# Moving the softmax shares' copies from ScalarE to GpSimd, starting the key and query splits one tile earlier, and giving the folded weights their own buffer

## The chip, the cores and the metric

The kernel runs on one core of a Trainium2 chip. The metric is device time in microseconds (us) of the whole program: the median of several runs. TensorE (PE) multiplies and transposes, VectorE (DVE) and ScalarE (ACT) read its results from PSUM, GpSimd (POOL) works on SBUF only, and nearly all transfers are issued by SyncE (SP), one after the other in program order.

## The reference

Three layers follow each other. The change lies in the work done during the first one.

```python
# 1: attention, B=4, H=8, S=1152, D=64; two queries are averaged into one
q_pool = q.reshape(B, H, S // 2, 2, D).mean(axis=3)
scores = scale * q_pool @ k^T
attn = exp(scores - max) / (sum + 1e-9)
x = (attn @ v) rearranged to (B, 576, 512)
# 2: four single-head causal attentions ("experts") on x, the best two per token mixed
ye = softmax(causal(scale * (x wq_e)(x wk_e)^T)) @ (x wv_e) @ wo_e
out = sum of the two chosen experts, weighted
# 3: gate = sigmoid(causal depthwise convolution of out, 5 taps)
result = (gate * (out @ w_val)) @ w_out
```

Everything is float32. A product that must keep more than the short float format holds is done with each operand split into a high part and a low part (the rest), both in the format that TensorE multiplies fast; those are the "splits" below.

## The kernel before

**Stage 1** is the first layer. It runs over 16 pairs of heads; a pair has nine tiles of 128 query rows in two units: unit 0 has the tiles `(u, i)` = (0, 0) to (0, 3), unit 1 has (1, 0) to (1, 4). One loop runs over all 144 tiles, and in a pass each engine gets work of several tiles: TensorE the scores of tile m+1 (L406) and the transposes of the probabilities of tile m-2 (L451); VectorE the row minimum of tile m+1 (L411); ScalarE the exponential of tile m (L417) and two of the three evacuations of the transposes (`pt`, L459), VectorE the third (L461). The transposes have two PSUM buffers, so the third group of a tile waits until ScalarE has emptied the first. Every engine works its instructions off in the order of the program.

When a unit's last tile is through, `shares` (L419) takes the reciprocals of the row sums (`rs`, L426 and L427) and spreads them into the tile `rm`, which has one buffer. One pass later `av` transposes `rm` (L438; a small matmul at L440 for the fifth tile's shares), ScalarE copies the result to `rb` (L472), TensorE runs 36 matmuls of probabilities by values (L476), and VectorE multiplies by `rb` (`xf`, L478). During these 36 matmuls the loop calls `between`, which also gives VectorE a stretch of decoding work (below).

**GpSimd's work in stage 1** comes from four sources, in this order within a pass: the list `late` (steps put off by an earlier pass, run at the head of the next), then one step of `prep`, then what `between` calls, then one step of `bgw`.

- `prep(n + 1)` makes the next pair's operands. It adds the two query halves (`qp`, L385), splits keys in three groups (`hlk`: high part L362, low part L363) and queries (`hlq`, L378 to L380). Its four steps run in four successive passes; low parts go to `late`. Then SP moves the splits into place (`kmove`, twelve transfers in three groups, and `qmove`, six).
- `av` puts the split of its result (`xt`, L485 and L481) on `late`; SP then stores it in `x_d`.
- `dense_weights` (iterator `bg`) decodes the third layer's weights on VectorE, with one addition on GpSimd (L103), and splits them on GpSimd into the tile `whl`, which SP stores in `w_d` (`w3_d`).
- `bgw` is `expert_weights` and then `folded_weights`: SP fetches a block of weights into `wst`, GpSimd splits it (L136, L138). `folded_weights` handles four blocks of the transposed output weights `wo_t`, into the same tile `whl` (L156, L157), stored in `wot_d`. The pool of `whl` has one buffer.

SP issues the load of pair n+2 (`kt`, `qt`, `vn`) in the pass of tile (1, 2). `kt` and `qt` have one buffer each.

**Stages 2 and 3** are the other layers. They begin at about 541 us and the change does not touch them.

Of the kernel before, what the change touches and what calls it, by code (L numbers as in the profile page):

```python
# [10 lines left out]
F32R = mybir.dt.float32r  # L11
I32 = mybir.dt.int32
AF = mybir.ActivationFunctionType
ALU = mybir.AluOpType
# [6 lines left out]
def tile_kernel(ctx, tc, q, k, v, w_gate, wq, wk, wv, wo, w_val, conv_w, w_out, wo_t, out):  # L21
    nc = tc.nc
    B, H, S, D = v.shape
    P = 128
# [9 lines left out]
    scale = 1.0 / math.sqrt(D)  # L34
    pe, act, dve, pool = nc.tensor, nc.scalar, nc.vector, nc.gpsimd
# [28 lines left out]
    def f(ap):  # L64
        return ap.bitcast(F32)
# [14 lines left out]
    HW = DM // 2  # L80
# [27 lines left out]
    def expert_weights(raws):  # L108

        ED = E * D  # L110
        todo = []
        for n, w in enumerate((wq, wk, wv)):
            for t in range(KT):
                dst = wqk if n < 2 else wvg
                cs = slice((n % 2) * ED, (n % 2) * ED + ED)
                todo.append((dst[0][:, t, cs], dst[1][:, t, cs], w[:, t * P:(t + 1) * P, :].rearrange("e p d -> p e d"), ED))
        for t in range(KT):
            todo.append((wvg[0][:, t, ED:], wvg[1][:, t, ED:], w_gate[t * P:(t + 1) * P, :], E))
        for g in range(EP):
            todo.append((wos[0][:, g, :], wos[1][:, g, :], wo[2 * g:2 * g + 2].rearrange("two d m -> (two d) m"), DM))  # L120
        bufs = {}

        def fetch(j):
            if j < len(todo):
                hi, lo, src, width = todo[j]
                st = bufs[j] = raws.tile([P, DM], F32, name="wst")[:, 0:width]
                nc.sync.dma_start(st if len(src.shape) == 2 else st.rearrange("p (e d) -> p e d", e=E), src)

        fetch(0)
        yield  # L130
        yield
        for j, (hi, lo, src, width) in enumerate(todo):
            fetch(j + 1)
            yield
            st = bufs.pop(j)
            pool.tensor_copy(hi, st)  # L136
            yield
            pool.tensor_tensor(out=lo, in0=st, in1=f(hi), op=ALU.subtract)  # L138

    def folded_weights(stage, raws):  # L140

        bufs = {}

        def fetch(t):
            if t < KT:
                bufs[t] = raws.tile([P, DM], F32, name="wst")[:, 0:HW]
                nc.sync.dma_start(bufs[t], wo_t[t * P:(t + 1) * P, :])

        fetch(0)
        yield  # L150
        for t in range(KT):
            fetch(t + 1)
            yield
            raw = bufs.pop(t)
            whl = stage.tile([P, 2, HW], F32R, name="whl")
            pool.tensor_copy(whl[:, 0], raw)  # L156
            pool.tensor_tensor(out=whl[:, 1], in0=raw, in1=f(whl[:, 0]), op=ALU.subtract)  # L157
            late.append(lambda t=t, whl=whl: nc.sync.dma_start(f(wot_d[:, t]), f(whl)))
            yield

    def dense_weights(stage, raws):

        craw = stage.tile([P, KT, KC, 2], I32, name="craw")
        cw64 = conv_w.bitcast(I32).rearrange("k (t p two) -> p t k two", p=P, two=2)
        for t in range(KT):
            nc.sync.dma_start(craw[:, t], cw64[:, t])
        big = [(n, t, c, w[t * P:(t + 1) * P, c:c + HW].bitcast(I32)) for n, w in enumerate((w_val, w_out)) for t in range(KT) for c in (0, HW)]
        bufs = {}

        def fetch(j):  # L170
            if j < len(big):
                bufs[j] = raws.tile([P, 2 * HW], I32, name="wraw")
                nc.sync.dma_start(bufs[j], big[j][3])

        fetch(0)
        yield True
        yield from decode(stage, craw.rearrange("p t k two -> p (t k) two"), KT * KC, cw.rearrange("p t k -> p (t k)"))
        for j, (n, t, c, src) in enumerate(big):
            fetch(j + 1)
            w32 = yield from decode(stage, bufs.pop(j).rearrange("p (m two) -> p m two", two=2), HW)  # L180
            whl = stage.tile([P, 2, HW], F32R, name="whl")
            pool.tensor_copy(whl[:, 0], w32)
            pool.tensor_tensor(out=whl[:, 1], in0=w32, in1=f(whl[:, 0]), op=ALU.subtract)
            late.append(lambda n=n, t=t, c=c, whl=whl: nc.sync.dma_start(f(w3_d[n][:, t, :, c:c + HW]), f(whl)))
            yield
# [116 lines left out]
    with ExitStack() as s1:  # L302
# [20 lines left out]
        own = sums_p.tile([P, P], F32, name="own")  # L323
# [12 lines left out]
        pairs = [(b, hp) for b in range(B) for hp in range(H // 2)]  # L336
        data = {}

        def load(n):
            b, hp = pairs[n]  # L340
            kt = nat.tile([P, C * P], F32, name="kt")
            nc.sync.dma_start(kt, k[b, hp])
            qt = nat.tile([P, 2, SQ], F32, name="qt")
            nc.sync.dma_start(qt, q[b, hp])
            vn = v_p1.tile([P, 2, C, D], F32, name="vn")
            nc.sync.dma_start(vn, v[b, 2 * hp:2 * hp + 2].rearrange("h (p c) d -> p h c d", p=P))
            data[n] = [qt, kt, vn]

        late = []
# [69 lines left out]
        def shares(m):  # L419

            n, u, i, _ = tiles[m]
            k = len(UNITS[u])
            if i == k - 1:
                rs = st_p.tile([P, 5], F32, name="rs")[:, 0:k]
                rm = rss[n, u] = rb_p.tile([P, 3, P], F32, name="rm")
                dve.tensor_scalar(rs, sums[(2 * n + u) % len(sums)][:, 0:k], 1e-9, None, op0=ALU.add)  # L426
                dve.reciprocal(rs, rs)  # L427
                both = rs[:, 0:4].rearrange("p (h t) -> p t h", h=2)[:, :, :, None].to_broadcast([P, 2, 2, D])
                act.activation(rm[:, 0:2].rearrange("p t (h d) -> p t h d", d=D), both, AF.Copy)
                if u == 1:  # L430
                    act.activation(rm[:, 2], own, AF.Copy, scale=rs[:, 4:5])

        def spread_shares(n, u):

# [107 lines left out]
        for m in range(-1, M + LAG + 4):  # L542
# [22 lines left out]
                fill = proj(xh[0], 0) + fill  # L565
            if 0 <= m < M:
                n, u, i, _ = tiles[m]
                if (u, i) == (0, 1) and n + 1 < len(pairs):
                    preps = prep(n + 1)
                if (u, i) == (1, 2) and n + 2 < len(pairs):  # L570
                    load(n + 2)
                if m == 5:
                    bg, bgw = dense_weights(d_p, raw_p), chain(expert_weights(raw_p), folded_weights(d_p, raw_p))
# [3 lines left out]
            for what, g in ((0, 0), (1, 0), (0, 1), (1, 1), (0, 2), (1, 2)) if burst else ((0, 0), (0, 1), (1, 0), (0, 2), (1, 1), (1, 2)):  # L577
                if what == 0:
                    if 0 <= m - LAG < M:
                        transp(m - LAG, g)  # L580
                    if m >= M:
                        now2, late2[:] = late2[:], []
                        if fill:
                            fill.pop(0)[1]()
                        for a in now2:
                            a()
                        if urgent:
                            urgent.pop(0)()
                        if not fill and late2:
                            for a in late2:  # L590
                                a()
                            late2.clear()
                    if g == 1:
                        if m in (0, 1):
                            begin[m]()
                        if 0 <= m < M and m not in done:
                            expo(m)
                        if m in (2, 3):
                            begin[m]()
                    if g == 2:  # L600
                        if 0 <= m - 1 < M:
                            shares(m - 1)
                        if preps:
                            preps.pop(0)()
                elif 0 <= m + 1 < M:
                    scores(m + 1, g)
# [60 lines left out]
    with ExitStack() as s2l:  # L667
# [157 lines left out]
        def ahead(n):  # L825
            return (WORK[steps[n][2]][0] if n < len(steps) else 0) + (WORK[steps[n - LAG][2]][1] if LAG <= n < len(steps) + LAG else 0)
# [34 lines left out]
        for n in range(len(steps) + LAG):  # L861
            if n < len(steps):
                b, g, i = s = steps[n]
# [36 lines left out]
            t = 0.0  # L900
            left = 5 - n % 5
            own = [ahead(m) for m in range(n, n + left)]
# [71 lines left out]
    with ExitStack() as s3:  # L974
# [5 lines left out]
        both = gs_p.tile([P, KT, 2, 2 * SQ], F32R, name="gs")  # L980
# [95 lines left out]
```

## Time and profile before

| what | value |
|---|---|
| median of 3 runs | 824.21 us (824.21 to 825.62) |
| the profiled execution, its own time | 824.22 us |
| its span, first to last instruction | 822.4 us |
| PE, DVE, ACT, POOL busy | 94%, 67%, 59%, 35% of the span |
| mean granted TensorE clock | 0.992 of full speed |

The profiled execution is as long as the median, and 1.8 us of it lie outside the span. "Busy" is an average over the three stages; which engine sets the pace at a given moment is read from the waits.

### The profile page before, as it was taken

Reading aid. Unit: us, or ns where it says so; the run is one execution under the profiler, and the core shown is the slowest. Engines: PE = TensorE matmul, PEld = TensorE weight load, DVE = VectorE, ACT = ScalarE, POOL = GpSimd, SP = SyncE. Lnnn points to the kernel's source line nnn. Section 1 sums busy time; section 2 is a strip of 40 time slices with the busy share of each in tenths; the row PEclk is TensorE's granted clock in tenths of the full one; section 3 lists DMA queues with packets and bytes.
Section 4 is the critical chain, followed back from the end, with each engine's and each line's share of the span. In section 5 each row is a group of like instructions: output and inputs, shape, how many; then the busy total and the mean of one; then the engine's idle time right before and its main releaser. Section 6 shows DMA issues by size and latency. Waiting matters only on the chain.

```text
span 822.4 us, 14720 instructions
## 1 busy us (share of the span) xinstructions
PE 774.1 (94%) x5348; PEld 629.6 (77%) x5348; DVE 548.8 (67%) x998; ACT 489.2 (59%) x1072; POOL 290.2 (35%) x372
## 2 busy tenths in 40 slices
PE   5999999997999999999999999998999999988998
PEld 4777777775777776786777777887998989876887
DVE  4577777776677777566556645526569889897840
ACT  5676677564665676666666756624455464647542
POOL 3463763844546345244144240002222222220000
PEclk9999999999999999999999999998999999999999
DMA  7767778666696595773764857067345464810212
GB/s 228 170 199 221 203 205 246 174 206 178 190 274 170 174 271 135 197 217 89 215 162 119 230 125 253 15 153 202 88 91 180 106 203 116 234 71 1 77 65 89
DMA packets 86295, 134.49 MB, mean 164 GB/s; under 512 B 21584, under 2 KB 58960, under 8 KB 86224
## 3 DMA queue, kind: packets, MB, share of 16 engines
q1 hardware_dynamic: 86224, 133.57, 57.6%
q8 instruction: 42, 0.69, 0.4%
q14 instruction: 29, 0.24, 0.1%
HBM read 53.37 MB, written 21.76 MB: 91 GB/s over the span
## 4 chain that ended last, share of the span: by engine, by line
PE 65%; DVE 13%; ACT 12%; DMA 5%; SPq 2%; issue 2%; POOL 0%; ACTq 0%; DVEq 0%
PE t L476 17%; PE s L406 12%; PE t L451 10%; ACT p L417 6%; PE a L231 6%; PE o L992 6%; DVE nm L411 5%; PE a L262 4%; PE a L782 3%; ACT pt L459 2%; DVE pt L461 2%; PE s L684 2%; DMA xh<-x_d 2%; PE a L649 2%; PE a L756 1%
## 5 line engine op out<-in xcount | busy, mean ns | idle before, releaser
L451 PE MATMUL t<-ident,p 128*128 128x128 f32 x1296 | 207.6, 280 | 17.9 <-ACT pt L459 15.2
L411 DVE TENSOR_REDUCE nm<-s 128x1 f32<-128x1152 f32 x144 | 194.1, 1348 | 28.7 <-PE s L406 21.8
L459 ACT ACTIVATE pt<-t 128x384 f32<-128x384 f32 x288 | 132.3, 488 | 134.7 <-PE t L451 133.4
L451 PEld LDWEIGHTS t<-ident,p 128*128 128x128 f32 x1296 | 151.7, 142 | 65.3 <-ACT pt L459 29.4
L417 ACT ACTIVATE p<-s,nm 128x1152 f32<-128x1152 f32 x144 | 176.2, 1224 | 37.7 <-DVE nm L411 33.5
L476 PE MATMUL t<-pt,vn 128*64 128x320 f32 (+1 forms) x1152 | 146.8, 408 | 0.0
L406 PE MATMUL s<-ka,qst 128*128 128x384 f32 x480 | 129.6, 373 | 13.3 <-ACT ka L523 6.9
L406 PE MATMUL s<-kb,qst 128*128 128x384 f32 x480 | 132.4, 368 | 2.0 <-ACT p L417 1.4
L461 DVE COPY pt<-t 128x384 f32<-128x384 f32 x144 | 80.4, 558 | 75.4 <-PE t L451 72.9
L476 PEld LDWEIGHTS t<-pt,vn 128*64 128x64 f32 x1152 | 80.0, 137 | 54.2 <-issue 2.7
L406 PEld LDWEIGHTS s<-ka,qst 128*128 128x128 f32 x480 | 78.5, 194 | 21.6 <-ACT p L417 8.7
L406 PEld LDWEIGHTS s<-kb,qst 128*128 128x128 f32 x480 | 77.4, 191 | 5.1 <-ACT p L417 2.0
L720 POOL TENSOR_TENSOR p<-p,sm 128x512 f32<-128x512 f32 (+3 forms) x32 | 40.2, 1255 | 114.3 <-DVE sm L718 85.2
L231 PE MATMUL a<-xh,wqk 128*128 128x288 f32 x384 | 59.7, 306 | 2.5 <-DVE pt L734 2.1
L478 DVE TENSOR_TENSOR xf<-t,rb 128x256 f32<-128x256 f32 (+1 forms) x32 | 14.6, 457 | 68.1 <-PE t L476 67.6
L485 POOL CAST xt<-xf 128x256 fp32r<-128x256 f32 (+1 forms) x32 | 13.6, 424 | 129.0 <-DVE xf L478 128.9
L231 PEld LDWEIGHTS a<-xh,wqk 128*128 128x128 f32 x384 | 54.5, 194 | 4.1 <-DVE pt L734 2.5
L363 POOL TENSOR_TENSOR hlk<-kt,hlk 128x384 fp32r<-128x384 f32 x45 | 45.4, 1010 | 2.2
L705 ACT ACTIVATE p<-s,nm 128x256 f32<-128x256 f32 (+3 forms) x64 | 33.1, 524 | 21.7 <-DVE nm L694 21.7
L385 POOL TENSOR_TENSOR qp<-qt 128x576 f32<-128x576 f32 x15 | 21.5, 1431 | 64.4 <-DMA qt<-in_q_dram 58.7
L204 DVE SCALAR_TENSOR_TENSOR gp<-x,cw,gp 128x572 f32<-128x572 f32 (+3 forms) x48 | 40.7, 849 | 2.6 <-ACT gp L803 2.1
L694 DVE TENSOR_REDUCE nm<-s 128x2 f32<-128x512 f32 (+4 forms) x40 | 32.4, 811 | 1.4
(170 smaller groups left out, 1063.0 us busy)
## 6 DMA issues: line engine op xcount, KB each, us to landing
ka<-hlk SPq DMA_DIRECT2D x90, 192.0 KB, 3.2
kb<-hlk SPq DMA_DIRECT2D x90, 192.0 KB, 3.7
vn<-in_v_dram SPq DMA_DIRECT2D x16, 576.0 KB, 7.8
xh<-x_d SPq DMA_DIRECT2D x16, 576.0 KB, 7.0
k<-hl SPq DMA_DIRECT2D x32, 288.0 KB, 4.9
kt<-in_k_dram SPq DMA_DIRECT2D x15, 576.0 KB, 5.4
qt<-in_q_dram SPq DMA_DIRECT2D x15, 576.0 KB, 6.5
x_d<-xt SPq DMA_DIRECT2D x16, 320.0 KB, 2.5
```

What stands on the lines that cost most here:

```text
L204: dve.scalar_tensor_tensor(out=gp[:, n:], in0=x[:, 0:SQ - n], scalar=cw[:, m, c:c + 1], in1=gp[:, n:], op0=ALU.mult, op1=ALU.add)
L231: pe.matmul(ps[:, 0:HQ], lhsT=wqk[wi][:, t, cs], rhs=xh[:, t, xi, qsl], start=o == 0, stop=o == len(ops) - 1)
L363: late.append(lambda: pool.tensor_tensor(out=hlk[:, 1, gs], in0=kt[:, gs], in1=f(hlk[:, 0, gs]), op=ALU.subtract))
L406: pe.matmul(ps[:, 0:GW], lhsT=a, rhs=c, start=o == 0, stop=o == len(ops) - 1)
L411: dve.tensor_reduce(d["nm"], d["s"][:, :, 0:GW], axis=AX.XY, op=ALU.min)
L417: act.activation(d["p"], d["s"][:, :, 0:GW], AF.Exp, bias=d["nm"], scale=-1.0, accum_out=sums[(2 * n + u) % len(sums)][:, i:i + 1])
L451: pe.transpose(ps[:, j * P:(j + 1) * P], p[:, g, j * P:(j + 1) * P], ident)
L459: act.activation(dst, src, AF.Copy)
L461: dve.tensor_copy(dst, src)
L476: pe.matmul(ps[64 * h:64 * h + 64, 0:N], lhsT=vn[:, h, j, :], rhs=pt[:, j, h, :], start=j == 0, stop=j == C - 1)
L720: pool.tensor_tensor(out=pv, in0=pv, in1=sm[:, :, None].to_broadcast([P, 2, w]), op=ALU.mult)
L992: pe.matmul(ps[:, 0:w], lhsT=hl[xi][:, kt, t * P - a:(t + 1) * P - a], rhs=end3["wo3"][:, kt, wi, c:c + w], start=o == 0, stop=o == len(op ...
```

## The change

It has three parts.

1. `shares` no longer spreads the reciprocals on ScalarE. It puts a function at the very head of `late`, so that GpSimd does the spreading (a copy for four tiles' shares, a multiplication for the fifth's) as the first thing of the next pass.
2. `prep` starts in the pass of a pair's tile (0, 0) and no longer in that of (0, 1), so each of its four steps, and the transfers behind them, stand one pass earlier in the program.
3. `folded_weights` writes to a tile of its own, `fhl`, and has two more empty steps per block, so its four blocks are spread over 16 passes and no longer over eight.

```diff
@@ folded_weights
-            whl = stage.tile([P, 2, HW], F32R, name="whl")
+            whl = stage.tile([P, 2, HW], F32R, name="fhl")
             pool.tensor_copy(whl[:, 0], raw)
             pool.tensor_tensor(out=whl[:, 1], in0=raw, in1=f(whl[:, 0]), op=ALU.subtract)
             late.append(lambda t=t, whl=whl: nc.sync.dma_start(f(wot_d[:, t]), f(whl)))
+            yield
+            yield
             yield
@@ shares
                 both = rs[:, 0:4].rearrange("p (h t) -> p t h", h=2)[:, :, :, None].to_broadcast([P, 2, 2, D])
-                act.activation(rm[:, 0:2].rearrange("p t (h d) -> p t h d", d=D), both, AF.Copy)
-                if u == 1:
-                    act.activation(rm[:, 2], own, AF.Copy, scale=rs[:, 4:5])
+
+                def copies():
+                    pool.tensor_copy(rm[:, 0:2].rearrange("p t (h d) -> p t h d", d=D), both)
+                    if u == 1:
+                        pool.tensor_scalar(rm[:, 2], own, rs[:, 4:5], None, op0=ALU.mult)
+
+                late.insert(0, copies)
@@ loop over the tiles
-                if (u, i) == (0, 1) and n + 1 < len(pairs):
+                if (u, i) == (0, 0) and n + 1 < len(pairs):
                     preps = prep(n + 1)
```

What the instruction order becomes is seen at three places. The lines of the changed kernel are numbered 2 to 6 higher.

On ScalarE, at the end of a unit 1 (the first pair's), there stood before:

```order
L429 ACTIVATE rm<-rs 128x256
L431 ACTIVATE rm<-own,rs 128x128
L459 ACTIVATE pt_440<-t 128x6x64 x2
L417 ACTIVATE p,sums_144<-s,nm 128x1152
L472 ACTIVATE rb<-t 128x320
```

and there stands now:

```order
L419 ACTIVATE p,sums_144<-s,nm 128x1152
L465 ACTIVATE pt_440<-t 128x6x64 x2
L419 ACTIVATE p,sums_144<-s,nm 128x1152
L478 ACTIVATE rb<-t 128x320
L419 ACTIVATE p,sums_144<-s,nm 128x1152
```

The evacuations `pt` now follow the exponential directly; the two `rm` rows are gone.

On GpSimd, where the first pair ends and the second begins, there stood before:

```order
L485 CAST xt_397<-xf_396 128x256
L481 TENSOR_TENSOR xt_397<-xf_396,xt_397 128x256
L136 CAST wqk_91<-wst 128x256
L138 TENSOR_TENSOR wqk_92<-wst,wqk_91 128x256
L385 TENSOR_TENSOR qp<-qt 128x576
L362 CAST hlk<-kt 128x384
L103 TENSOR_TENSOR cw<-cw,dec_626 128x20
L136 CAST wqk_91<-wst 128x256
L363 TENSOR_TENSOR hlk<-kt,hlk 128x384
L485 CAST xt_598<-xf_597 128x320
L378 TENSOR_SCALAR qp<-qp 128x576
L379 CAST hlq<-qp 128x576
```

and there stands now:

```order
L136 CAST wqk_91<-wst 128x256
L387 TENSOR_TENSOR qp<-qt 128x576
L364 CAST hlk<-kt 128x384
L138 TENSOR_TENSOR wqk_92<-wst,wqk_91 128x256
L433 COPY rm<-rs 128x256
L435 TENSOR_SCALAR rm<-own,rs 128x128
L365 TENSOR_TENSOR hlk<-kt,hlk 128x384
L380 TENSOR_SCALAR qp<-qp 128x576
L381 CAST hlq<-qp 128x576
L103 TENSOR_TENSOR cw<-cw,dec_633 128x20
L136 CAST wqk_91<-wst 128x256
L382 TENSOR_TENSOR hlq<-qp,hlq 128x576
```

The query addition, the first key split and a weight split now stand ahead of the two `rm` rows of unit 1, and the first key's low part and the query splits stand ahead of the decoding's additions (L103).

On GpSimd, at the second block of folded weights, there stood before:

```order
L379 CAST hlq<-qp 128x576
L156 CAST whl<-wst 128x256
L157 TENSOR_TENSOR whl<-wst,whl 128x256
L481 TENSOR_TENSOR xt_2215<-xf_2214,xt_2215 128x320
L380 TENSOR_TENSOR hlq<-qp,hlq 128x576
L362 CAST hlk<-kt 128x384
L363 TENSOR_TENSOR hlk<-kt,hlk 128x384
L362 CAST hlk<-kt 128x384
L156 CAST whl<-wst 128x256
L157 TENSOR_TENSOR whl<-wst,whl 128x256
L363 TENSOR_TENSOR hlk<-kt,hlk 128x384
L182 CAST whl<-dec_2251 128x256
```

and there stands now:

```order
L382 TENSOR_TENSOR hlq<-qp,hlq 128x576
L491 CAST xt_2222<-xf_2221 128x320
L364 CAST hlk<-kt 128x384
L487 TENSOR_TENSOR xt_2222<-xf_2221,xt_2222 128x320
L365 TENSOR_TENSOR hlk<-kt,hlk 128x384
L364 CAST hlk<-kt 128x384
L365 TENSOR_TENSOR hlk<-kt,hlk 128x384
L156 CAST fhl<-wst 128x256
L157 TENSOR_TENSOR fhl<-wst,fhl 128x256
L433 COPY rm<-rs 128x256
L184 CAST whl<-dec_2258 128x256
```

No block of folded weights stands between the key and query splits of the pair any more; the second block comes behind the last of them.

## Rows read from the trace of the kernel before

**Rows 1.** Waits of TensorE, 60 to 535 us: total, times, longest.
```profile
PE t L451 <- ACT pt L459: 12.9, 27, 1.4
PE s L406 <- DMA ka<-hlk: 4.5, 2, 3.1
PE t L451 <- DVE xf L478: 2.3, 2, 1.4
```

**Rows 2.** Timeline, one unit's shares: start, duration, instruction [idle before it, releaser].
```profile
307.67 0.43 DVE L426 TENSOR_SCALAR rs<-sums 128x5 f32<-128x5 f32 x1
...
308.36 0.42 ACT L429 ACTIVATE rm<-rs 128x256 f32<-128x256 f32 x1
...
308.68 0.39 ACT L431 ACTIVATE rm<-own,rs 128x128 f32<-128x128 f32 x1
308.97 0.85 ACT L459 ACTIVATE pt<-t 128x384 f32<-128x384 f32 x2
...
309.49 0.55 PE L451 MATMUL t<-ident,p 128*128 128x128 f32 x3 [0.52 <-ACT pt L459]
...
310.58 0.38 PE L438 MATMUL t<-ident,rm 128*128 128x128 f32 x2
```

**Rows 3.** Timeline, GpSimd and TensorE around the folded weights.
```profile
189.38 0.55 POOL L156 CAST whl<-wst 128x256 fp32r<-128x256 f32 x1 [3.80 <-DMA w_d<-whl]
...
194.47 0.55 PE L451 MATMUL t<-ident,p 128*128 128x128 f32 x3 [1.45 <-DVE xf L478]
...
199.76 1.01 POOL L363 TENSOR_TENSOR hlk<-kt,hlk 128x384 fp32r<-128x384 f32 x1
...
202.16 0.58 PE L406 MATMUL s<-ka,qst 128*128 128x384 f32 x2 [1.40 <-DMA ka<-hlk]
...
205.87 0.69 PE L406 MATMUL s<-ka,qst 128*128 128x384 f32 x2 [3.13 <-DMA ka<-hlk]
...
233.35 0.55 PE L451 MATMUL t<-ident,p 128*128 128x128 f32 x3 [0.87 <-DVE xf L478]
```

**Rows 4.** Busy time in 205 to 210 us; PEclk is the granted clock.
```profile
205.00:210.00 5.00, 4.13 (x18) 3.93 (x19) 2.20 (x3) 2.19 (x4) 1.72 (x3) 0.66 1.02 257
```

**Rows 5.** Groups of GpSimd instructions by shape: busy us, mean ns of one.
```profile
L378 POOL TENSOR_SCALAR qp<-qp 128x576 f32<-128x576 f32 x15 | 24.8, 1652 | 1.1
...
L485 POOL CAST xt<-xf 128x256 fp32r<-128x256 f32 x16 | 6.3, 396 | 47.3 <-DVE xf L478 47.3
L138 POOL TENSOR_TENSOR wqk<-wst,wqk 128x256 fp32r<-128x256 f32 x8 | 5.9, 738 | 0.2
```

**Rows 6.** Timeline, end of the first pair.
```profile
45.44 0.38 PE L438 MATMUL t<-ident,rm 128*128 128x128 f32 x2
...
46.40 1.41 POOL L385 TENSOR_TENSOR qp<-qt 128x576 f32<-128x576 f32 x1 [3.85 <-DMA qt<-in_q_dram]
...
47.75 0.53 POOL L362 CAST hlk<-kt 128x384 fp32r<-128x384 f32 x1
```

**Rows 7.** Timeline of a later pair: last key split, next load, its first use.
```profile
323.99 1.00 POOL L363 TENSOR_TENSOR hlk<-kt,hlk 128x384 fp32r<-128x384 f32 x1
...
331.62 0.51 SPq L344 DMA_DIRECT2D qt<-in_q_dram  x1
...
337.92 1.41 POOL L385 TENSOR_TENSOR qp<-qt 128x576 f32<-128x576 f32 x1 [6.02 <-DMA qt<-in_q_dram]
...
341.51 0.55 PE L451 MATMUL t<-ident,p 128*128 128x128 f32 x3 [0.36 <-ACT pt L459]
```

**Rows 8.** Timeline, first block of folded weights and that unit's shares.
```profile
172.95 0.38 PE L438 MATMUL t<-ident,rm 128*128 128x128 f32 x2
...
175.58 0.50 POOL L156 CAST whl<-wst 128x256 fp32r<-128x256 f32 x1 [10.24 <-DMA wst<-in_moe_wo_t_dram]
```

**Rows 9.** The instructions of line 426: shortest/median/longest in ns, first and last start.
```profile
L426 DVE TENSOR_SCALAR rs<-sums x32: 158/433/1368, 25.8 to 534.8; 128x4 f32<-128x4 f32 x16, 128x5 f32<-128x5 f32 x16
```

**Rows 10.** Timeline, that line's longest instruction; a decoding step and `xf`.
```profile
274.47 1.42 POOL L385 TENSOR_TENSOR qp<-qt 128x576 f32<-128x576 f32 x1 [7.71 <-DMA qt<-in_q_dram]
274.55 1.37 DVE L426 TENSOR_SCALAR rs<-sums 128x5 f32<-128x5 f32 x1
...
312.05 0.41 DVE L105 SCALAR_TENSOR_TENSOR dec<-dec,dec 128x256 f32<-128x256 int32 x1
...
316.24 0.49 DVE L478 TENSOR_TENSOR xf<-t,rb 128x320 f32<-128x320 f32 x1 [1.23 <-PE t L476]
```

## The prediction

> **What bounds the kernel now.** The page comes first: TensorE is nearly always busy, and no other engine comes near it. So a change in stage 1 is worth what it takes from, or adds to, TensorE's idle time. The second view is therefore the list of TensorE's waits in stage 1. There are three kinds [rows 1]: 12.9 us in 27 waits of the transposes for ScalarE's evacuation, 4.5 us in two waits for moved keys, 2.3 us in two waits for `xf`. The third view, the timeline, says where they lie.
>
> The first kind sits in the one pass of a unit in which ScalarE spreads the shares. In [rows 2] the two `rm` instructions start at 308.36 and 308.68, the evacuations only at 308.97, and TensorE, which needs the first one's buffer, idles 0.52 us before 309.49. ScalarE also waits there for the reciprocals.
>
> The other two kinds lie between 190 and 234 us and have one origin. GpSimd's split of a folded block found `whl` still being stored, and stood idle 3.80 us ahead of 189.38 [rows 3]. The pair's remaining splits queue behind it: the last low part of the keys runs at 199.76, its transfers follow, and TensorE waits 1.40 and 3.13 us for `ka`. Twice `xf` came late instead, 1.45 and 0.87 us, with decoding on VectorE entangled with the crowded GpSimd.
>
> **What the change does, part by part.** All durations are of the profiled execution, whose 824.22 us are the median's 824.21.
>
> *Copies leave ScalarE.* The evacuation can start 308.97 - 308.36 = 0.6 us earlier, more than the 0.52 us that TensorE idles, so the wait should vanish. Later instructions do not take it back: 36 long matmuls follow, during which the other engines have slack. Over the 27 waits that is -12.9 us; the first two units lie ahead of the window and are priced apart.
>
> *Copies arrive on GpSimd.* The trace has no such copy there. Nearest is the cast of the same 128x256 shape, 0.40 us; from above the bound is TensorScalar, 1.65 us for 576 columns, so 0.73 us for 256 [rows 5]. I take 0.40. The 128-column multiplication is 0.37 us by TensorScalar's rate, up to 0.5 with a fixed part. The shares are ready when ScalarE now starts `rm`, 308.36; TensorE transposes `rm` at 310.58, and 0.52 earlier after the change, so at 310.06 [rows 2]. With GpSimd free the copy is done at 308.8 and the multiplication at 309.3. That is hidden, with about 0.8 us to spare at either bound. If the cover is gone, every us goes straight to TensorE, since the 36 matmuls queue behind the transposes.
>
> *Is GpSimd free then?* Unit 1's copies stand behind the query addition and the first key split, which wait for the next load. Where the load is late, the copies are late. In a later pair the last low part ends at 325.0, the load of `qt` is issued at 331.62, and the addition starts at 337.92, when it has landed [rows 7]. After the change the first low part, the query scaling and the query cast (1.0 + 1.65 + 0.67 us) run ahead of the long matmuls, where GpSimd now idles, and no longer behind them. So I estimate the whole chain of splits, moves and load some 3.3 us earlier, the addition at 334.6, and addition plus split done by 336.6. The next shares are due 32.0 us after 308.36 (309.49 to 341.51 is one period [rows 2, 7]), at 340.4, or about 339.5 with the gains. So it is free there.
>
> *The first pair is different.* Its load is not moved: SP issues without a pause up to it. `qt` lands at 46.40, as before [rows 6]. Now the copies of that unit stand behind the addition (1.41), the split (0.53) and a weight split (0.74 [rows 5]): 46.40 + 1.41 + 0.53 + 0.74 + 0.40 = 49.5 us, where TensorE wants them at 45.44. That is +4.1 us. The pairs behind it then have that much more time for their loads.
>
> *A stall can cost clock too.* After the waits at 202 and 205 us the granted clock was 0.66 on average for 5 us, so for most of them at the lower of its two levels (1.2 and 2.4 GHz) [rows 4]: 5 x (1 - 0.66) = 1.7 us lost. With those waits gone this comes back, -1.7 us; the new stall of 4.1 us may cost the like, between 0 and 1.7, and I take +1.0.
>
> *Folded weights.* `fhl` is not shared, and the blocks stand four passes apart, behind the splits instead of between them. So the waits of [rows 3] should go: -(1.40 + 3.13 + 1.45 + 0.87) = -6.9 us. The first block's fetch comes late, however: it landed at 175.58 while TensorE transposed `rm` at 172.95 [rows 8], and that block now stands ahead of a pair of copies. With the load 3.3 us earlier the fetch lands at 172.3. Cast, subtraction (0.74 [rows 5]) and copy follow, 0.50 + 0.74 + 0.40 us, to 173.9, where TensorE, itself some 0.35 us earlier, wants `rm` at 172.6: +1.3 us. Bounds: 0, and 4.6 if the fetch lands no earlier.
>
> *Contention.* Line 426 takes 0.16 us at best and 1.37 us at 274.55, when GpSimd's addition had started just before and ended with it [rows 9, 10]: VectorE stood still meanwhile. GpSimd's new work lies in the 4 us behind the shares. VectorE's decoding starts at 312.05, 3.7 us after them, and may be pushed by up to half an us; `xf` had 1.23 us to spare at 316.24 [rows 10]. I take +0.5 us in all.
>
> The Trainium skill, SBUF — State Buffer, section Who interferes with whom, says that GpSimd and certain VectorE instructions, TensorScalar among them, lock one port pair for a whole instruction and the later one blocks fully. By that rule the trace agrees (1.37 against 0.16 us), and the rule speaks against the change, as it adds GpSimd instructions; what it could cost at most is the third rival.
>
> Sum: -12.9 - 6.9 - 1.7 + 4.1 + 1.0 + 1.3 + 0.5 = -14.6 us, so 824.2 - 14.6 = 809.6, in round terms **809.5 us**.
>
> **The rivals.**
>
> 1. *Loads come no earlier in the early pairs* (0.13). Weight fetches and splits fill GpSimd and SP up to some 175 us, and the chain may move less than I estimate. Then unit 1's copies are late not once but in five pairs: 4.1 us at [rows 6], 4.6 at [rows 8], and I estimate half of that, 2 us, in the three between. That is 3.3 + 6 = 9.3 us more: 818.9. For it: both landings shown are behind TensorE's need. Against it: the first stall by itself gives the later loads 4 us.
> 2. *The other side: the copies wait for the load in every pair* (0.06). Unit 1's copies stand behind an addition that waits for a transfer. In the pair of [rows 7] they would be done at 337.92 + 1.41 + 0.5 + 0.85 = 340.7 even with the old landing, and TensorE wants them at about 342. But the earlier moves may collide with the load on the transfer engines; a load that lands 3.1 us later than before, instead of 3.3 earlier, costs 1.8 us a pair, 27 us over 15 pairs, and with the first stall and its clock the sum is -21.5 + 5.1 + 1.8 + 27 = +12.4: 837. It decides from 1 us a pair on (15 us). Against it: the moves need no more transfers than before.
> 3. *The decoding becomes late* (0.05). By the 0.87 us of [rows 3] in each of some 15 remaining stretches of decoding, 13 us: 822.5. Against it: 1.23 us of slack.
> 4. *The wait at the shares is not ScalarE's copies but the next thing in line* (0.06): the evacuation still starts late since `rs` also holds up VectorE's row minimum, and only half of the 12.9 us is won: 816.
>
> The forecast as worked out has 0.70. Its own range is 804 to 814: down to 804 if the first stall costs no clock and the folded block nothing and TensorE's small waits go as well (1.0 + 1.3 + 0.5, and some 3 us), up to 814 if the copies take 0.73 us and the folded block 4.6. The range that should hold 8 in 10 reaches to the fourth rival and part of the first: 803 to 818. About 0.2%, 1.6 us, is what a measurement tells from no change. Faster: the forecast, rivals 1 and 4, and most of 3: 0.91. Same 0.03, slower 0.06.
>
> **What would show it.** In the changed profile: TensorE's waits for `pt` in stage 1 down from 12.9 us to under 2; no wait for `ka` near 200 us and no low clock there; a new wait of TensorE for `rm` of about 4 us near 46 us, and one of 0 to 2 us near 173; a period of about 31.1 us per pair in later pairs, where it is 32.0; query additions that start some 3 us earlier against the shares. Waits for `rm` in many pairs would make me wrong by rival 1 or 2, waits for `xf` by rival 3, a period still near 32 by rival 4.

## The result, and the profile after

The changed kernel takes 804.85 us (median of 4 runs, 802.95 to 807.51) where the kernel before, run beside it, takes 824.91: a ratio of 0.974 with a 95% interval of 0.9705 to 0.9775 (the two medians alone give 0.976), 20 us less. The forecast was 809.5 us, range 803 to 818. The profiled execution is the longest of the four: 807.51 us, span 805.7 against 822.4 before, so the two traces below differ by 16.7 us.

The page shows the moved work. Before, GpSimd was busy 290.2 us in 372 instructions and ScalarE 489.2 us in 1072.

```profile
PE 769.3 (95%) x5348; PEld 627.6 (78%) x5348; DVE 542.0 (67%) x998; ACT 473.7 (59%) x1024; POOL 310.6 (39%) x420
```

The waits of TensorE from 60 to 535 us, total, times, longest, stand against [rows 1]. ScalarE's evacuation (`pt`) fell from 12.9 us to 0.3, the waits for moved keys and for `xf` are gone, and a wait for `rm`, now GpSimd's, has come in:

```profile
PE t L444 <- POOL rm L433: 3.0, 2, 2.2
PE t L446 <- POOL rm L435: 0.3, 1, 0.3
PE t L457 <- ACT pt L465: 0.3, 1, 0.3
```

The timeline at the end of the first pair answers to [rows 6]. The query addition starts as before, when `qt` has landed, and three instructions run ahead of the copy. TensorE is idle for 3.16 us and transposes `rm` at 49.42, where it was 45.44:

```profile
46.45 1.40 POOL L387 TENSOR_TENSOR qp<-qt 128x576 f32<-128x576 f32 x1 [4.18 <-DMA qt<-in_q_dram]
47.79 0.53 POOL L364 CAST hlk<-kt 128x384 fp32r<-128x384 f32 x1
48.29 0.73 POOL L138 TENSOR_TENSOR wqk<-wst,wqk 128x256 fp32r<-128x256 f32 x1
48.97 0.39 POOL L433 COPY rm<-rs 128x256 f32<-128x256 f32 x1
49.35 0.60 POOL L435 TENSOR_SCALAR rm<-own,rs 128x128 f32<-128x128 f32 x1
...
49.42 0.69 PE L444 MATMUL t<-ident,rm 128*128 128x128 f32 x2 [3.16 <-POOL rm L433]
```

The same place in stretches of 5 us (after the engines' busy time the granted clock, DMA share, GB/s): the stall ends in the first of them, and in the next the clock is 0.50, which is the lower level, 1.2 GHz, for the whole stretch. The last row is the stretch of [rows 4], which has the full clock now:

```profile
45.00:50.00 5.00, 1.84 (x12) 1.24 (x10) 4.11 (x9) 1.64 (x3) 3.55 (x6) 0.88 0.66 219
50.00:55.00 5.00, 5.00 (x21) 2.52 (x22) 0.00 (x0) 1.64 (x3) 4.84 (x6) 0.50 0.61 147
55.00:60.00 5.00, 5.00 (x36) 3.12 (x33) 0.49 (x1) 0.98 (x2) 1.44 (x4) 0.94 0.65 161
205.00:210.00 5.00, 4.97 (x35) 4.16 (x34) 4.43 (x7) 4.65 (x10) 2.38 (x4) 1.00 0.99 310
```

At the first folded block, which answers to [rows 8], the block stands ahead of the copy, and TensorE waits:

```profile
177.78 0.40 POOL L156 CAST fhl<-wst 128x256 fp32r<-128x256 f32 x1 [0.62 <-DMA wst<-in_moe_wo_t_dram]
178.26 0.72 POOL L157 TENSOR_TENSOR fhl<-wst,fhl 128x256 fp32r<-128x256 f32 x1
178.93 0.59 POOL L433 COPY rm<-rs 128x256 f32<-128x256 f32 x1
...
179.57 0.44 PE L444 MATMUL t<-ident,rm 128*128 128x128 f32 x2 [2.19 <-POOL rm L433]
```

**The balance.** How far the transposes of `rm` lie behind those of before, place by place, shows where the time went in this profile. At the first unit they are 1.15 us late, a difference of the start-up. Then +2.8 us at the first pair's stall (to 3.98), +2.9 by the clock behind it (60.14 before, 67.00 after: 6.86), +0.8 at a wait at 115.11, +2.5 at 179.57, and about -8.6 in the two units that held the folded blocks' waits (from 6.82 to -1.61 and from -1.84 to -3.52, less some 1.5 us of ordinary gain). Together +1.5. The last of these transposes is 15.7 us earlier than before (525.11 against 540.78), so **some 17 us** were won in ordinary units; the other 1.0 us of the span's 16.7 lies behind that transpose, in layers that the change does not touch. The term had been -12.9.

**Where the rest of the ordinary gain was.** An ordinary unit 0 before the change shows it. `rs` runs beside GpSimd's key split and takes 0.69 us instead of 0.16, ScalarE waits 0.33 us for the reciprocals, copies, and evacuates only then:

```profile
322.45 1.01 POOL L363 TENSOR_TENSOR hlk<-kt,hlk 128x384 fp32r<-128x384 f32 x1
...
322.79 0.69 DVE L426 TENSOR_SCALAR rs<-sums 128x4 f32<-128x4 f32 x1
322.82 0.82 PE L451 MATMUL t<-ident,p 128*128 128x128 f32 x6
...
323.45 0.61 PE L406 MATMUL s<-kb,qst 128*128 128x384 f32 x2
...
323.73 0.42 ACT L429 ACTIVATE rm<-rs 128x256 f32<-128x256 f32 x1 [0.33 <-DVE rs L427]
...
324.05 0.85 ACT L459 ACTIVATE pt<-t 128x384 f32<-128x384 f32 x2
...
324.57 0.55 PE L451 MATMUL t<-ident,p 128*128 128x128 f32 x3 [0.51 <-ACT pt L459]
```

The same unit after:

```profile
315.58 0.82 PE L457 MATMUL t<-ident,p 128*128 128x128 f32 x6
...
316.06 0.40 POOL L433 COPY rm<-rs 128x256 f32<-128x256 f32 x1 [1.53 <-DVE rs L429]
316.11 0.87 ACT L465 ACTIVATE pt<-t 128x384 f32<-128x384 f32 x2
...
316.20 0.62 PE L408 MATMUL s<-kb,qst 128*128 128x384 f32 x2
...
316.66 0.55 PE L457 MATMUL t<-ident,p 128*128 128x128 f32 x3
```

From the six transposes to the next three it was 324.57 - 322.82 = 1.75 us and is 316.66 - 315.58 = 1.08: 0.67 us are won, though the row of before shows only 0.51 us of idle time. The score matmuls ahead of them tell why: undisturbed, the transposes start 316.66 - 316.20 = 0.46 us after them, 0.16 us before their row ends (0.62 us). The rows of matmuls overlap, and idle time is counted from the end of the row ahead, so this wait looks 0.16 us shorter than what it costs. Over the 27 waits that is some 4 us, and 12.9 + 4 is the 17 of the balance. The same distance, from a unit's score matmuls to the next transposes, can be read at nearly every unit: it was 0.68 to 2.07 us before (30 units read) and is 0.45 to 0.47 now (27 units). What lay above 0.46 adds up to 17.7 us before, and to nothing now. A pair in the later part takes 30.8 us instead of 32.0 (303.33 to 334.12; 310.58 to 342.60 before).

### The profile page after: what moved, and what is told of

Its sections match the earlier page's. It is cut to its first block, busy times and chain, and to the rows that moved or that the text cites. A ratio compares the mean times of both kernels' runs of the same rounds, so it can differ in the third digit from the quotient of the medians.

```text
span 805.7 us, 14797 instructions
## 1 busy us (share of the span) xinstructions
PE 769.3 (95%) x5348; PEld 627.6 (78%) x5348; DVE 542.0 (67%) x998; ACT 473.7 (59%) x1024; POOL 310.6 (39%) x420
## 4 chain that ended last, share of the span: by engine, by line
PE 71%; DVE 10%; DMA 6%; ACT 4%; SPq 4%; POOL 3%; issue 2%; ACTq 0%; DVEq 0%; POOLq 0%
PE t L482 17%; PE s L408 16%; PE t L457 13%; PE a L233 6%; PE o L998 6%; PE a L264 4%; DVE nm L413 3%; ACT p L419 3%; PE a L788 3%; DMA xh<-x_d 2%; PE s L690 2%; PE a L655 2%; PE a L762 1%; DVE pt L467 1%; SPq L513 1%
## 5 line engine op out<-in xcount | busy, mean ns | idle before, releaser
L457 PE MATMUL t<-ident,p 128*128 128x128 f32 x1296 | 205.5, 278 | 2.5 <-ACT pt L465 2.4
L482 PE MATMUL t<-pt,vn 128*64 128x320 f32 (+1 forms) x1152 | 149.2, 413 | 0.0
L408 PEld LDWEIGHTS s<-ka,qst 128*128 128x128 f32 x480 | 77.9, 193 | 16.7 <-ACT p L419 8.9
L433 POOL COPY rm<-rs 128x256 f32<-128x256 f32 x32 | 12.9, 404 | 67.9 <-PE t L457 45.9
```

Source lines behind the costliest of these rows:

```text
L408: pe.matmul(ps[:, 0:GW], lhsT=a, rhs=c, start=o == 0, stop=o == len(ops) - 1)
L457: pe.transpose(ps[:, j * P:(j + 1) * P], p[:, g, j * P:(j + 1) * P], ident)
L482: pe.matmul(ps[64 * h:64 * h + 64, 0:N], lhsT=vn[:, h, j, :], rhs=pt[:, j, h, :], start=j == 0, stop=j == C - 1)
```

## The experiments

The time fell by more than the sum, so two things were open. Did the surplus belong to the copies that left ScalarE (part 1), or to the earlier splits (part 2), which also free VectorE at the shares? And what did the new stalls cost? The median times of the kernel before were 826.64, 826.99 and 825.67 us in the three sets of runs; ratios are against those.

**Each part alone.** `e1_copies_only` has part 1:

```diff
-                act.activation(rm[:, 0:2].rearrange("p t (h d) -> p t h d", d=D), both, AF.Copy)
-                if u == 1:
-                    act.activation(rm[:, 2], own, AF.Copy, scale=rs[:, 4:5])
+
+                def copies():
...
+                late.insert(0, copies)
```

> The kernel before with the copies on GpSimd alone (splits start at tile (0, 1), folded blocks share whl). Theory A: taking the copies off ScalarE gives TensorE more than its idle rows say, some 0.6 us per unit and 18 us over 30 units, since a later pair then lasts 30.8 us; the waits around 190 to 234 us stay, and there is no stall at 46 us, since the copies stand ahead of the query addition: about 806 us. Theory B: the copies give only what the idle rows say (12.9 us, 0.45 us per unit, a pair lasts 31.1 us) and the rest of the gain comes from the earlier splits: about 811 us.

821.79 us, ratio 0.9935 [0.9909, 0.9962]: far less of a gain than either figure. The gain per pair is there (317.07 to 348.01 us: 30.94), but it is given back: the waits of TensorE from 60 to 535 us are now for `rm`, and in the longest, 6.3 us at 205.37, the copy stands behind splits that ran late and behind a folded block that waited for the store of `whl`: the wait for the keys has moved to the copies. At that transpose TensorE is 17.6 us later than in the kernel before (187.78 there).

```profile
PE t L442 <- POOL rm L431: 16.1, 7, 6.3
PE t L444 <- POOL rm L433: 0.7, 3, 0.3
```

`e2_early_only` has part 2:

```diff
-                if (u, i) == (0, 1) and n + 1 < len(pairs):
+                if (u, i) == (0, 0) and n + 1 < len(pairs):
```

> The kernel before with the earlier splits alone (copies on ScalarE, whl shared). Theory A: nothing on TensorE's path waits for them in a later pair, a pair still lasts 32.0 us: 824 us, less 1 at most. Theory B: with the splits done earlier VectorE's reciprocals meet GpSimd less often, ScalarE gets them earlier, a pair lasts about 31.7 us: about 819 us.

820.51 us, 0.992 [0.9897, 0.9944]. The number is near theory B's, but its mechanism is not there: later pairs are not shorter (32.3 us). The gain lies at the folded blocks, where the stretch that took 72.3 us before (172.95 to 245.29) takes 68.3.

`e3_fhl_only` has part 3:

```diff
-            whl = stage.tile([P, 2, HW], F32R, name="whl")
+            whl = stage.tile([P, 2, HW], F32R, name="fhl")
...
+            yield
+            yield
```

> The kernel before with the own buffer and the wider spacing of the folded blocks alone. Theory A: the waits of 6.9 us between 190 and 234 us and 1.7 us of low clock go, nothing else changes: about 816 us. Theory B: the same 816 us. Rival for this part: the blocks' splits crowd GpSimd at another place and half of it comes back: 820 us.

819.4 us, 0.9911 [0.9881, 0.9941]. The folded stretch takes 64.6 us (175.10 to 239.70), and later pairs are as before (32.02). This is the fold term by itself: 7.2 us, by the interval 5 to 10, where the sum had 8.6. The waits for `ka` are gone, but one wait for `xf` is left (1.09 us at 196.07), so the waits for `xf` did not all come from the shared tile. What the tile and what the wider spacing does was not told apart.

**Parts by twos.** `e4_copies_fhl` is the change without part 2:

```diff
-                if (u, i) == (0, 0) and n + 1 < len(pairs):
+                if (u, i) == (0, 1) and n + 1 < len(pairs):
```

> The change without the earlier splits: copies on GpSimd and own buffer. Theory A: 18 and 8.5 us are won and there is no stall at 46 us and no low clock behind it, as the copies stand ahead of the query addition: about 798 us, 7 less than the change. Theory B: the earlier splits carried 5 us of the gain, which are missing here, against the 7 us of the stall: about 803 us.

818.41 us, 0.9891 [0.985, 0.9932]: both figures were wrong by 15 us or more. There is no stall at 46 us, as expected, and later pairs take 30.96 us, but TensorE waits 10.9 us for `rm` in 8 places. In the longest the load of the first folded block lands late, and the block stands right ahead of the copies; in two others (at 80.30 and 147.93) it is a split of the experts' weights whose load lands late. The rows are the timeline and the stretch that follows, nearly all of it at the lower clock:

```profile
183.98 0.64 POOL L156 CAST fhl<-wst 128x256 fp32r<-128x256 f32 x1 [8.62 <-DMA wst<-in_moe_wo_t_dram]
...
185.50 0.59 POOL L433 COPY rm<-rs 128x256 f32<-128x256 f32 x1
...
186.14 0.69 PE L444 MATMUL t<-ident,rm 128*128 128x128 f32 x2 [3.50 <-POOL rm L433]
```

```profile
185.00:190.00 5.00, 3.81 (x14) 2.04 (x16) 1.85 (x4) 1.64 (x3) 4.92 (x8) 0.52 0.38 108
```

`e9_copies_early` is the change without part 3 (`whl` shared, no added `yield`):

```diff
-            whl = stage.tile([P, 2, HW], F32R, name="fhl")
+            whl = stage.tile([P, 2, HW], F32R, name="whl")
...
-            yield
-            yield
```

> The change without the own buffer and the wider spacing: copies and earlier splits, folded blocks in whl again. If the earlier splits by themselves already take the folded blocks out of the keys' way (alone they left half of the loss between 172 and 245 us), the third part is worth some 4 us: about 809 us. If the copies also queue behind the blocks that wait for whl, TensorE waits for them there as it did without the earlier splits (up to 6 us at one unit): about 815 us.

820.92 us, 0.9933 [0.9912, 0.9954]: worse than both figures, mostly for one wait. The block waits for the store of the shared tile, the copy stands behind it, and TensorE idles 11.34 us, then works in part at the lower clock (0.73 from 205 to 210 us):

```profile
202.93 0.40 POOL L156 CAST whl<-wst 128x256 fp32r<-128x256 f32 x1 [5.24 <-DMA wot_d<-whl]
203.40 0.72 POOL L157 TENSOR_TENSOR whl<-wst,whl 128x256 fp32r<-128x256 f32 x1
204.07 0.40 POOL L431 COPY rm<-rs 128x256 f32<-128x256 f32 x1
...
204.52 0.69 PE L442 MATMUL t<-ident,rm 128*128 128x128 f32 x2 [11.34 <-POOL rm L431]
```

`e10_early_fhl` is the change without part 1 (the copies stay on ScalarE):

```diff
-                def copies():
...
-                late.insert(0, copies)
+                act.activation(rm[:, 0:2].rearrange("p t (h d) -> p t h d", d=D), both, AF.Copy)
+                if u == 1:
+                    act.activation(rm[:, 2], own, AF.Copy, scale=rs[:, 4:5])
```

> The change without its first part: earlier splits and own buffer, copies on ScalarE. Theory A: the folded blocks' waits are gone, a later pair lasts 32 us again, and there is no stall at 49 us: about 816 us; the first part, on top of the other two, is then worth some 11 us, where alone it gave 5. Theory B: without meeting GpSimd the reciprocals reach ScalarE earlier and a pair lasts 31.7 us: about 812 us.

816.31 us, 0.9888 [0.9863, 0.9913], as theory A expected; later pairs take 31.6 to 32.7 us. The waits for `pt` are back, and nothing else is in the list from 60 to 535 us:

```profile
PE t L453 <- ACT pt L461: 9.2, 15, 1.4
```

So part 1 on top of the other two is worth 0.9888 - 0.973 = 0.016, some 13 us, give or take 3; by itself it is worth 5, give or take 2.

**The price of ScalarE's time.** `e11_copy_twice` is the kernel before with the 256-column copy made twice:

```diff
                 act.activation(rm[:, 0:2].rearrange("p t (h d) -> p t h d", d=D), both, AF.Copy)
+                act.activation(rm[:, 0:2].rearrange("p t (h d) -> p t h d", d=D), both, AF.Copy)
```

> The kernel before with the 128x256 copy of the shares done twice on ScalarE, nothing else. Theory A: ScalarE's time at this place goes to TensorE one to one: 0.3 to 0.4 us for each of 32 units, 10 to 13 us more, about 838 us. Rival: part of it is hidden behind VectorE's row minimum, which ends close behind: half of that, about 832 us.

836.77 us, 1.014 [1.01, 1.018]: 11.1 us more (by the interval 8 to 15), 0.35 per unit for a copy of 0.41, as theory A had it. ScalarE's time at this place goes to the end nearly whole.

**The new stalls.** `c0_change` is the change again, as the measure for these:

> The change itself once more, so that the variants beside it are compared on one chip: 0.974 of before, about 805 us, with TensorE waiting some 3 us for the copies near 49 us and some 2 us near 180 us, and a low clock for some 5 us behind the first of these.

804.25 us, 0.9728 [0.9699, 0.9758]. The stalls are smaller here than in the first profile, and than expected: 1.62 us at 49.06, with a clock of 0.66 from 50 to 55 us, and 0.57 us at 175.57.

```profile
50.00:55.00 5.00, 5.00 (x27) 2.42 (x28) 0.61 (x1) 1.64 (x3) 4.79 (x6) 0.66 0.64 154
PE t L444 <- POOL rm L433: 2.2, 2, 1.6
```

The first row is the stretch, the second the wait for `rm` from 40 to 535 us. The first unit's `rm` transpose lies at 30.90 here and at 29.66 in the first profile, while the transpose behind the load of `qt` lies at 49.06 and 49.42: TensorE started later and found less to wait for. From the first `rm` transpose to the last it takes 489.9 us here and 495.5 there, and nearly all of the difference lies at these stalls. So the 9 us of new stalls in the balance are one profile's; this one has about 4.

`e5_first_pair_act` leaves the first pair's copies on ScalarE:

```diff
-                late.insert(0, copies)
+                if n == 0:
+                    act.activation(rm[:, 0:2].rearrange("p t (h d) -> p t h d", d=D), both, AF.Copy)
+                    if u == 1:
+                        act.activation(rm[:, 2], own, AF.Copy, scale=rs[:, 4:5])
+                else:
+                    late.insert(0, copies)
```

> The change, but the first pair's copies stay on ScalarE. Theory A: the first pair's stall (4.0 us) and the low clock behind it (2.9 us) are a plain loss; both go and nothing else moves: 7 us less than the change, about 798 us. Theory C: that stall gave the later loads their head start; without it TensorE waits for the copies at several later unit 1s, 1 to 3 us each, and half or more comes back: 801 to 805 us.

802.14 us, 0.9696 [0.9665, 0.9726]. The stall near 47 us is gone and the clock there is full, but the 7 us that theory A wanted are not seen in the time: the median is 2.1 us lower, and the intervals overlap. Time and waits are those of theory C: the pairs behind it start earlier and have less time for their loads, and waits stand at 110.34 (1.0 us) and 174.91 (2.1); the second costs clock (0.66 from 175 to 180 us). The wait list from 40 to 535 us:

```profile
PE t L449 <- POOL rm L433: 3.1, 2, 2.1
PE t L462 <- ACT pt L470: 0.6, 2, 0.4
PE t L487 <- DVE pt L472: 0.4, 1, 0.4
PE t L451 <- POOL rm L435: 0.2, 1, 0.2
```

`e6_six_pairs_act` does so for six pairs (`n < 6`):

> The change, but the copies of the first six pairs, in which GpSimd also splits the experts' weights, stay on ScalarE. Theory A: the stalls near 49, 115 and 180 us go (10 us with the clock), but ten more units keep ScalarE's copies in TensorE's path at 0.6 us: about 4 to 5 us less than the change, 800 to 801 us, and slower than with the first pair alone on ScalarE. Theory C: late copies in those pairs cost more than ScalarE's: faster than with the first pair alone.

805.92 us, 0.9743 [0.9716, 0.9771], not the 800 to 801 us of theory A, and not faster than e5, as theory C would have it. No wait for `rm` is left, but in twelve units TensorE waits again behind ScalarE's copies (waits for `pt` of 3.3 us in 7 from 40 to 535 us). `e7_first_act_fold_later` is e5 with one more empty step ahead of the first folded block:

```diff
         fetch(0)
+        yield
         yield
         for t in range(KT):
```

> As the one with the first pair's copies on ScalarE, and the folded blocks one pass later, so that the first block stands behind a unit 1's copies and no longer ahead of them. Theory A: the wait of some 2 us for the copies near 175 us goes too: 2 us less than without it, about 796 us. Theory C: the copies are late there for the load's sake and not for the block's: no difference.

804.26 us, 0.9732 [0.9705, 0.976]: no gain over e5, as theory C wanted, but for another reason. The wait at 175 us is gone, so it was the block's, and a later block has taken its place: it waits until the store of the block before it has freed the tile, and stands ahead of the next pair's copies.

```profile
204.53 0.40 POOL L157 CAST fhl<-wst 128x256 fp32r<-128x256 f32 x1 [0.88 <-DMA wot_d<-fhl]
...
206.13 0.44 PE L450 MATMUL t<-ident,rm 128*128 128x128 f32 x2 [1.75 <-POOL rm L434]
```

`e8_four_units_act` is e5 with two more units on ScalarE, the two whose copies came late in e5:

```diff
-                if n == 0:
+                if n == 0 or (n, u) in ((2, 1), (4, 1)):
```

> The change, but four units keep their copies on ScalarE: both of the first pair, and unit 1 of the third and of the fifth pair, where the copies were still late with the first pair alone on ScalarE (TensorE waited 1.3 us near 110 us and 2.4 us near 175 us, and 2 us of low clock followed). Theory A: a late copy is worth what the wait and the clock show, so 5.5 us go and two units pay 0.6 us again: 4 us less than with the first pair alone, a ratio of about 0.965. Theory C: the lateness only moves to the next unit 1, as with the folded blocks one pass later: no difference, 0.970.

800.45 us, 0.9702 [0.9673, 0.9731]. The list from 40 to 535 us has no `rm` any more, and from its first to its last `rm` transpose it takes 487.3 us, the least of all (before 512.3, the change 495.5 and 489.9 in its two profiles). Its ratio can't be told from that of e5 or of the change; theory C had that number, but not by its mechanism, since no copy is late any more:

```profile
PE t L462 <- ACT pt L470: 1.3, 4, 0.4
```

**The distance, run by run.** What belongs to ScalarE's copies is seen without the stalls in the distance read above, from a unit's score matmuls to the next transposes:

| run | units read | distance, us | sum above 0.46, us |
|---|---|---|---|
| before | 30 | 0.68 to 2.07 | 17.7 |
| `e10_early_fhl`, copies on ScalarE | 30 | 0.68 to 2.02 | 15.2 |
| `e11_copy_twice` | 30 | 1.13 to 2.14 | 30.0 |
| `e6_six_pairs_act`, 12 units on ScalarE | 30 | 0.44 to 1.60 | 5.4 |
| `e1_copies_only`, copies on GpSimd | 26 | 0.44 to 0.46 | 0 |
| the change | 27 | 0.45 to 0.47 | 0 |

The excess is there where the copies are on ScalarE, grows with a second copy, and is gone where they are on GpSimd, with or without the other two parts. In e10 every unit 0 that was read has 0.68 to 0.78, an idle time too short for the list of waits; so the list has 9.2 us there and the distances 15.2.

**The table.** C is the copies, E the earlier splits, F the folded blocks' tile: C 0.9935, E 0.992, F 0.9911, C+E 0.9933, C+F 0.9891, E+F 0.9888, all three 0.973. The single gains add to 2.3%, and all three together give 2.7%; but no two of them give clearly more than the better one alone.

## Why the prediction was right, point by point

The direction, the mechanism and the range held. The time came out 4.7 us under the predicted one (20 us less instead of 14.6), within the forecast's own range of 804 to 814, but near its low end and not by the road given for it: 804 was to need a first stall without loss of clock and a folded block without a stall, and both cost more than taken. In the profiled execution two misses of some 4 us nearly cancel, the ordinary units' gain (17 instead of 12.9) and the stalls with their clock; that the sum of that profile comes so close (16.7) is in part luck.

- **Copies leave ScalarE: right, and mis-sized.** The term "over the 27 waits that is -12.9 us" was taken from TensorE's idle time; it measured some 17 us (17.7 by the distances). The idle time of overlapping matmul rows leaves out 0.16 us per wait. The other number that stood in the same step, ScalarE's evacuation starting 0.6 us earlier, was the better one: times 30 units it is 18 us. A pair takes 30.8 us where 31.1 was forecast; of the 1.2 us won, 1.1 come with the copies alone (`e1_copies_only`, 30.94). `e11_copy_twice` shows the same price from the other side. That "ScalarE also waits there for the reciprocals" hardly holds for the unit of [rows 2], where its copy starts at 308.36, as soon as ScalarE is free (308.31); it holds for the unit 0 shown above (0.33 us).
- **Copies on GpSimd.** The 256-column copy takes 0.40 us, as taken; the 128-column multiplication takes 0.60, above the 0.37 to 0.5 assumed from TensorScalar's rate per column. It stayed hidden in ordinary units.
- **GpSimd is free then: right.** In a later pair the load of `qt` is issued at 320.62 and the addition starts at 327.16, some 2.5 to 3 us earlier against the shares than in [rows 7] (3.3 estimated); the copy starts at 332.44, 3.4 us after addition and split are done.
- **The first pair: right as to place and cause.** `qt` landed at 46.45 and the copy was done at 49.36 (46.40 and 49.5 forecast), and `rm` moved by 3.98 us (+4.1). But 1.15 of these are the later start, so the stall itself cost 2.8, and 1.2 in the profile of `c0_change`: `qt` lands there at 46.11, nearly the same time, and stalls a TensorE that is later by itself less, which the sum left out. **Its clock** cost 2.9 us, above the +1.0 taken and the bound of 1.7, and 1.8 in `c0_change`: [rows 4] held a shorter fall, since the whole stretch from 50 to 55 us is at the lower level in the first profile.
- **Folded weights: right.** -8.6 us for the two waits, `xf` and the clock, forecast -6.9 and -1.7. The first block's stall was 2.5 us (0.57 us of idle time in `c0_change`), within the bounds of 0 and 4.6 around +1.3. "One origin" is too strong: with the tile of its own alone (`e3_fhl_only`) one wait for `xf` stayed.
- **Contention: no cost.** The +0.5 went the other way. Line 426's 0.43 us median [rows 9] is now 0.16, the longest 0.47 (row below). In late pairs it is seen which part did it: from 290 us on, up to the last pair but one, `rs` of a unit 0 takes 0.68 to 0.70 us in the two runs with the copies on GpSimd but without the earlier splits (`e1_copies_only`, `e4_copies_fhl`) and 0.16 with both (the change, `c0_change`, `e9_copies_early`), and a late pair is 0.17 us longer without. With the earlier splits but the copies on ScalarE (`e2_early_only`, `e10_early_fhl`) single ones still take 1.3 us. So it takes both parts. By the rule in the Trainium skill, SBUF — State Buffer, section Who interferes with whom (GpSimd and some VectorE instructions exclude each other for a whole instruction) the trace agrees (0.69 us beside GpSimd's split at 322.45, 0.16 without one); I had read it as speaking against the change, and here it spoke for it.

```profile
L428 DVE TENSOR_SCALAR rs<-sums x32: 158/160/471, 25.9 to 519.1; 128x4 f32<-128x4 f32 x16, 128x5 f32<-128x5 f32 x16
```

**The rivals.** The first, loads that come no earlier in the early pairs, did not happen: the additions at 79.03, 112.17 and 141.69 start 2 to 5 us before TensorE wants `rm` (83.39, 114.3, 146.37), where in the same pairs before they started between 0.8 us ahead of it and 1.2 behind. Of the five places that it named, three have a wait: 3.2 and 2.2 us, which the forecast had too, and 0.8. Without part 2 (`e4_copies_fhl`, 818.41 us) eight units wait, but behind weight splits and the pair's own splits, and a unit 1's copies stand ahead of the query addition there; that this time is near the rival's 818.9 is chance. The second, waits in every pair, did not happen in any run: later pairs had 3.4 us in hand. The third fell with the waits for `xf` gone. The fourth fell with the wait for `pt`, 0.3 us, though its mechanism was real: `rs` did hold up ScalarE, and both came free together.

**What the sum didn't say** is how much the parts need each other. It priced all three together, as terms that add, and asked whether GpSimd is free only for the whole change; the runs show that the copies pay 13 us where GpSimd is on time and 5 where it isn't.

**Left open.** What the new stalls cost in the median run is not settled. The two profiles of the change have about 9 and 4 us of them, and e8, without any, is not clearly faster: the stretch of its profile is 2.6 us shorter than that of c0's, where the two profiles of the change differ by 5.5.

## What to carry to other kernels

To price work taken off an engine that others wait for, compare when the waiting instruction starts against an undisturbed pass; the idle time before overlapping matmuls was too small here, by 0.16 us at each wait. Work moved to another engine paid here only as far as everything queued ahead of it there was on time, so look for what is ahead of it in the program and waits for a transfer, and test the move together with the edits that make that engine punctual: alone it may seem worthless. Price a stall from more than one profile: that of the first pair was 3.16 us in one and 1.62 in the other. Repairing it returned less than its length, and late copies came in behind it, most likely because the later passes lost the head start that it had given their loads.

## What the runs showed of the hardware that was not expected

- A stall of TensorE of 3.16 us went with a granted clock of 0.88, 0.50 and 0.94 in the stretch of 5 us in which it ended and the two behind it, 2.9 us lost, nearly as much again. Shorter waits differed: after 2.19 us at 179.57 the clock stayed at 1.00, after 2.09 us in `e5_first_pair_act` and after 1.62 us in `c0_change` it was 0.66 for a stretch. What decided is open.
- GpSimd's multiplication of 128 columns by a share per partition took 0.60 us (median of 16), longer than its copy to 256 columns (0.40), which spreads four.
- The first `rm` transpose lay between 28.5 and 32.3 us in the profiles of these kernels, most of which do nothing different before it, so the stretch between two points inside the program compares better than spans.
